# Decay of the third group of chunks loaded and made ahead of the first FFN slot, in a buffer of its own

## The chip, the cores and the metric

The kernel runs on one core of a Trainium2 chip. The metric is the device time of one execution in microseconds (us); less is better. The engines are TensorE (PE in the rows), VectorE (DVE), ScalarE (ACT), GpSimd (POOL) and SyncE (SP), which issues most of the DMAs. Each runs its own row of instructions in order and waits for the others through semaphores.

## What is computed

Three steps follow each other: a gated linear attention, a dense feed-forward network with SiLU, and a second network in which each token goes to the one of eight experts that its gate prefers.

```
def _attn_ref(q, k, v, f_logit):                    # 4 batches, 8 heads, 768 tokens, 48 channels
    f = 1.0 / (1.0 + np.exp(-f_logit))
    for t in range(S):
        state = f[:, :, t, :, None] * state + np.einsum('bhd,bhe->bhde', k[:, :, t], v[:, :, t])
        y[:, :, t] = np.einsum('bhd,bhde->bhe', q[:, :, t], state)
def _moe_ref(x, w_in, w_out):                       # 3072 tokens, 384 channels, 2048 inside
    h = x @ w_in
    g = h * (1.0 / (1.0 + np.exp(-h)))
    return g @ w_out
def _moe2_ref(x, w_gate, w1, w2):                   # top 1 of 8 experts, 1024 inside
    logits = x @ w_gate
    expert_idx = np.argmax(logits, axis=1)
    ...
        out[mask] = gate_w[mask, None] * (np.maximum(xe @ w1[e], 0.0) @ w2[e])
```

The inputs and the result are fp32.

## The kernel before

**Tiling.** The 3072 tokens are 24 chunks of 128; six chunks are one batch. Every large product is made of three TensorE passes over operands that are split into a high and a low part (`_hi`, `_lo`), so each weight and each activation needs a cast on ScalarE (the high part, L226) and a subtraction on VectorE (the low part, L227). The first network's weights also go through a few shifts and masks on VectorE ahead of that (L199, L295 to L303: TENSOR_SCALAR and SCALAR_TENSOR_TENSOR rows on `in_cv`, `out_cv`). The raw weights come by L219, L221 and L222 (`out_raw`, `in_raw`).

**Attention of a chunk** is seven stages, `att0` to `att6`. `att0` makes the decay: a clamp on VectorE (L317), an exponential (L318) and a logarithm (L319) on ScalarE, together a softplus, and then the split `lfh`, `lfl` (L323, L324). `att1` sums it along the chunk by TensorE (`pl`), takes exponentials `ep`, `en` of it (L346 to L348) and makes `qpad`, `kpad` (L349, L350); it also sends the chunk's last row through DRAM (`ends`, L351) to have it as a column (`a_all`, L353). `att2` transposes (`pq`, `pk`, copied as `qt`, `kt`), `att3` makes the scores `sc` and masks them (`am`, L397, two halves of four heads), `att4` the output `py` and the update `pu`, with which VectorE carries the running `state` on (L453, L455), and `att5` transposes the output (`pt`) into `big` or `xt` (L474, L475), the input of the dense network.

**The dense network** works on groups of two or three chunks: the first group is chunks 0 and 1, the second 2 and 3, the third 4, 5 and 6, the fourth 7, 8 and 9. A group takes 16 slots, one for each 128 of the 2048 inner channels. A slot is `ph` (9 matmuls), its Tanh on ScalarE (`se`, L494), `sg` on VectorE (L496), `gh` on ScalarE (L504), `gl` on VectorE (L505), and two slots later `px`. So slots 0 to 15 are the first group's, with attention of later chunks between them. In the rows of the instructions, `se_0_530` is the Tanh of the first half of a slot.

**What sets the order.** A plan `at(slot, fn, ...)` says in which slot a piece is written; pieces before slot 0 have negative numbers. The order on TensorE is then kept as written. On the other engines and SyncE's queue a scheduler puts the instructions in order, by the order in which they are written and by a modelled time at which their inputs and buffers are there: a piece that is ready early by the model can be lifted far ahead of where it was written. The loads of the decay's input of chunks 0 to 3 have places of their own; from the third group on a group's chunks share one tile `in_f` of which there is one buffer: the next group's loads can go out when the last reader of the tile before is done. The Tanh's activation table is not the one that holds exponential and logarithm, so ScalarE loads a table (ACT_TABLE_LOAD) at each change.

`big` is a buffer of 12,288 bytes on each partition. It holds the inputs `xt0` of the first group, a row of zeros `zrow` from which GpSimd and SyncE fill a table in DRAM between slots 22 and 30, and later other tiles: the gate's turned rows `rt`, and an expert's activations `hh_h`.

The functions `load_chunk`, `att0`, `flip_rows` and the plan at the end of the kernel are what the change touches:

## Time and profile before

| | us |
|---|---|
| time, median of 3 runs (lowest, highest) | 857.92 (856.4, 859.5) |
| the profiled execution | 859.19 |
| its span, first to last instruction | 857.5 |
| TensorE busy in the span | 820.6 |
| VectorE, ScalarE, GpSimd busy | 488.1, 384.2, 109.3 |
| mean granted TensorE clock | 0.98 of full |

The profile is of one execution. TensorE's busy time is an upper figure, as its matmuls are pipelined and their ends are modelled. A granted clock of 1.00 is 2.4 GHz, 0.50 is 1.2 GHz. In a timeline a row is the start in us from the span's begin, the duration, the engine and line, the operation, the tiles written and read, and in brackets how long the engine had been idle before it and what ended that. Rows of one engine overlap slightly, so the distance from start to start is what an instruction takes of the engine.

### The profile page before, as it was taken

The numbers are of one execution on the slowest core, as the hardware profiler recorded it, in microseconds if no ns is written. First come the engines' busy times: TensorE is split into PE (matmuls) and PEld (weight loads), VectorE is DVE, ScalarE is ACT, GpSimd is POOL, SyncE is SP. The second block draws the span as 40 slices with busy tenths as digits, with TensorE's granted clock in tenths as the row PEclk, the third lists the DMA queues.
The fourth block names the chain that finished last, engine by engine and source line by source line (L and its number), as shares of the span: only waits on it lengthen the run. The fifth ranks groups of instructions, "written<-read, shape, count | busy, mean of one in ns | idle before, by whom it ended". The sixth has DMA issues, their size and how long they took to land.

```text
span 857.5 us, 15398 instructions
## 1 busy us (share of the span) xinstructions
PE 820.6 (96%) x5684; PEld 782.8 (91%) x5684; DVE 488.1 (57%) x1288; ACT 384.2 (45%) x803; POOL 109.3 (13%) x144
## 2 busy tenths in 40 slices
PE   6899899999999999999999999998999999999994
PEld 3789899989999999999999999998998999999994
DVE  5999875566655556566566556353455336336520
ACT  5665544353353453344445333355264435435520
POOL 2010000002002001001001001066201110110001
PEclk9699899999999999999999999998999999999998
DMA  9856774313244243353344323114182516525400
GB/s 202 172 150 164 188 227 121 65 38 96 71 99 106 59 101 102 75 103 102 74 94 103 74 56 104 44 39 157 48 298 67 172 61 196 170 79 181 162 26 27
DMA packets 166437, 95.94 MB, mean 112 GB/s; under 512 B 115692, under 2 KB 159965, under 8 KB 166352
## 3 DMA queue, kind: packets, MB, share of 16 engines
q1 hardware_dynamic: 162224, 83.80, 37.5%
q0 software_dynamic: 3280, 9.49, 3.0%
q10 hardware_dynamic: 848, 1.57, 0.6%
q8 instruction: 46, 0.75, 0.4%
q14 instruction: 39, 0.32, 0.1%
HBM read 75.61 MB, written 16.33 MB: 107 GB/s over the span
## 4 chain that ended last, share of the span: by engine, by line
PE 70%; DMA 10%; issue 6%; DVE 5%; ACT 5%; SPq 2%; POOL 1%; POOLq 0%; DVEq 0%; ACTq 0%
PE px L330 19%; PE ph L330 19%; PE po L330 8%; PE p L330 7%; PE py L330 5%; DMA out_dram<-o,oi 3%; DMA f<-in_f_logit_dram 2%; PE sc L330 2%; DMA w_raw<-in_moe_w_dram 2%; PE pl L330 1%; PE plt L330 1%; PE p_r L330 1%; PE pq L335 1%; PE po_r L330 1%; PE pk L335 1%
## 5 line engine op out<-in xcount | busy, mean ns | idle before, releaser
L494 ACT ACTIVATE se<-ph 128x384 f32<-128x384 f32 (+1 forms) x144 | 65.5, 455 | 170.2 <-PE ph L330 162.6
L330 PE MATMUL px<-out_lo,gh 128*128 128x384 f32 x384 | 136.7, 356 | 1.6 <-ACT gh L504 1.6
L496 DVE SCALAR_TENSOR_TENSOR sg<-se,ph 128x384 f32<-128x384 f32 (+1 forms) x144 | 72.9, 506 | 108.5 <-ACT se L494 106.0
L330 PE MATMUL px<-out_hi,gl 128*128 128x384 f32 x384 | 130.3, 339 | 1.2 <-DVE gl L505 1.2
L330 PE MATMUL px<-out_hi,gh 128*128 128x384 f32 x384 | 130.0, 338 | 0.0
L330 PE MATMUL ph<-xtl,in_hi 128*128 128x384 f32 (+1 forms) x384 | 125.8, 327 | 0.8 <-DVE xtl L475 0.8
L330 PE MATMUL ph<-xth,in_hi 128*128 128x384 f32 (+1 forms) x384 | 124.1, 323 | 0.0
L330 PE MATMUL ph<-xth,in_lo 128*128 128x384 f32 (+1 forms) x384 | 123.9, 323 | 0.0
L505 DVE TENSOR_TENSOR gl<-sg,gh 128x384 fp32r<-128x384 f32 (+1 forms) x144 | 79.6, 553 | 37.4 <-ACT gh L504 36.5
L504 ACT CAST gh<-sg 128x384 fp32r<-128x384 f32 (+1 forms) x144 | 68.6, 476 | 64.6 <-DVE sg L496 59.2
L330 PEld LDWEIGHTS px<-out_lo,gh 128*128 128x128 f32 x384 | 72.6, 189 | 4.2 <-ACT gh L504 2.3
L330 PEld LDWEIGHTS px<-out_hi,gl 128*128 128x128 f32 x384 | 72.8, 190 | 1.7 <-DVE gl L505 1.7
L330 PEld LDWEIGHTS ph<-xtl,in_hi 128*128 128x128 f32 x384 | 72.6, 189 | 1.1 <-DVE xtl L475 1.1
L330 PEld LDWEIGHTS ph<-xth,in_lo 128*128 128x128 f32 x384 | 72.6, 189 | 0.0
L330 PEld LDWEIGHTS px<-out_hi,gh 128*128 128x128 f32 x384 | 72.6, 189 | 0.0
L330 PEld LDWEIGHTS ph<-xth,in_hi 128*128 128x128 f32 x384 | 72.5, 189 | 0.0
L330 PE MATMUL po<-w_lo,hh 128*128 128x384 f32 (+6 forms) x200 | 67.8, 339 | 0.0
L330 PE MATMUL po<-w_hi,hh 128*128 128x384 f32 (+6 forms) x200 | 67.2, 336 | 0.0
L330 PE MATMUL po<-w_hi,hl 128*128 128x384 f32 (+6 forms) x200 | 67.2, 336 | 0.0
L226 ACT CAST w_hi<-w_raw 128x384 fp32r<-128x384 f32 x124 | 56.9, 513 | 21.6 <-DMA w_raw<-in_moe_w_dram 19.6
L330 PE MATMUL p<-xsl,w_hi 128*128 128x480 f32 (+6 forms) x168 | 58.5, 348 | 0.0
L330 PE MATMUL p<-xsh,w_hi 128*128 128x480 f32 (+6 forms) x168 | 58.4, 347 | 0.0
(240 smaller groups left out, 1528.4 us busy)
## 6 DMA issues: line engine op xcount, KB each, us to landing
w_raw<-in_moe_w_dram SPq DMA_DIRECT2D x64, 384.0 KB
xs<-big SPq DMA_DIRECT2D x8, 776.0 KB
out_again<-in_moe_w_out_dram SPq DMA_DIRECT2D x16, 384.0 KB
xe<-xs SPq DMA_DIRECT2D x7, 776.0 KB
out_raw<-in_moe_w_out_dram SPq DMA_DIRECT2D x13, 384.0 KB
f<-in_f_logit_dram SPq DMA_DIRECT2D x24, 192.0 KB
k<-in_k_dram SPq DMA_DIRECT2D x24, 192.0 KB
q<-in_q_dram SPq DMA_DIRECT2D x24, 192.0 KB
```

Of the source, the lines that this page charges most:

```text
L226: (keep(nc.scalar.copy) if key == ("w1", 1, 1) and RT > 1 else nc.scalar.copy)(hi[:, h], x)
L330: ins = nc.tensor.matmul(*a, **k)
L335: ins = nc.tensor.transpose(*a, **k)
L494: nc.scalar.activation(e, ph[:, :GT], AF.Tanh, scale=0.5)
L496: nc.vector.scalar_tensor_tensor(out=t, in0=e, scalar=1.0, in1=ph[:, :GT], op0=ALU.add, op1=ALU.mult)
L504: (nc.scalar.copy if g < GACT else nc.vector.tensor_copy)(hi, t)
L505: (nc.gpsimd if (g, i) < LOV else nc.vector).tensor_sub(lo, t, hi.bitcast(F32))
```

## The change

The loads of the third group's decay input move from the slot of its first chunk's loads (-3) to `F3 - 2` = -4, and its clamp, exponential and logarithm from `att0` of chunk 4 (slot 0) to `F3` = -2. They need room while `in_f` still holds chunks 0 and 2, 3. So `big` is cut to 4 x 384 words (6,144 bytes), and a new `side` of 388 + 3 x 384 words (6,160 bytes) holds the row of zeros and, behind it, the third group's three chunks. The tiles that took the place of `big` later take `side` (`rt`) or both (`hh_h`).

```diff
 WE = -6
 WS = -1
 PF = 22
+F3 = -2
 PFD = 1
 PW = (0, 0, 1, 1, 2, 2, 3, 3)
 GACT = 9
...
     qpads = [const.tile([P, H, 64], F32, name=f"qpad{i}") for i in range(2)]
     kpads = [const.tile([P, H, 64], F32, name=f"kpad{i}") for i in range(2)]
     wgc = const.tile([P, KC, E], F32, name="wgc")
-    big = late.tile([P, 6 * 512], F32R, tag="big", name="big")
+    big = late.tile([P, 4 * DM], F32R, tag="big", name="big")
+    side = late.tile([P, ROW + CPG * DM], F32, tag="side", name="side")
     xt0 = [big[:, i * 2 * DM : (i + 1) * 2 * DM].rearrange("p (r c t) -> p r c t", r=2, c=KC) for i in range(2)]
-    zrow = big[:, 4 * DM : 4 * DM + ROW].bitcast(F32)
-    spare = big[:, 5 * DM + 2 : 5 * DM + 3]
+    zrow = side[:, :ROW]
+    spare = side[:, DM + 2 : DM + 3]
+    f_third = side[:, ROW:].rearrange("p (r h d) -> p r h d", r=CPG, h=H)
     BANKS = {0: "haahhaaa", 1: "haahhaaa"}
 
     def use(n, i, name):
...
                 tag = {"f": "sg", "q": "gh", "k": "gh", "v": "gl"}[nm]
                 t = att.tile([P, H, D], F32, tag=tag, name=f"{nm}_{n}", bufs=BUFS[tag])
             elif nm == "f":
-                if n == 0 or n == starts[g] and g > 1:
+                if g == 2:
+                    fb[g] = f_third
+                elif n == 0 or n == starts[g] and g > 1:
                     fb[g] = att.tile([P, CPG, H, D], F32, tag="in_f", name=f"f_{n}")
                 t = fb[g][:, r] if g > 1 else fb[0][:, max(n - 1, 0)]
             else:
...
     ysb = {}
     xt = {}
 
+    def softplus(t):
+        nc.vector.tensor_scalar_max(t, t, FMIN)
+        nc.scalar.activation(t, t, AF.Exp, scale=-1.0)
+        nc.scalar.activation(t, t, AF.Ln, bias=1.0)
+
     def att0(n):
         f = loaded.pop(("f", n))
         g, _ = group_of[n]
-        if g < 2 or n == starts[g]:
-            t = f if g < 2 else fb[g][:, : sizes[g]]
-            nc.vector.tensor_scalar_max(t, t, FMIN)
-            nc.scalar.activation(t, t, AF.Exp, scale=-1.0)
-            nc.scalar.activation(t, t, AF.Ln, bias=1.0)
+        if g < 2:
+            softplus(f)
+        elif g > 2 and n == starts[g]:
+            softplus(fb[g][:, : sizes[g]])
         hi = att.tile([P, DM], F32R, name=f"lfh_{n}", **first_use(n, "lfh", "gl"))
         lo = att.tile([P, DM], F32R, name=f"lfl_{n}", **first_use(n, "lfl", "gl"))
         f2 = f.rearrange("p h d -> p (h d)")
...
         for c in range(KC):
             pe.transpose(pt[:, c * P : (c + 1) * P], r[:, c * P : (c + 1) * P], ident)
         if not turned_rows:
-            turned_rows.append(late.tile([P, 4, KC, P], F32, tag="big", name="rt"))
+            turned_rows.append(late.tile([P, 4, KC, P], F32, tag="side", name="rt"))
         rt = turned_rows[0][:, (starts[g] + t) % 4]
         nc.scalar.copy(rt.rearrange("p c t -> p (c t)"), pt[:, :DM])
         flipped[g, t] = pt, rt
...
         w = HEAD * P
         xt_hl = [att.tile([P, CPG, KC, P], F32R, tag=f"xt{x}", name=f"xe{x}_h", bufs=2) for x in "hl"]
         flat = [x.rearrange("p r c t -> p (r c t)") for x in xt_hl]
-        big = late.tile([P, 8 * DM], F32R, tag="big", name="hh_h")
+        bigs = [late.tile([P, 4 * DM], F32R, tag=x, name=f"hh_{x}") for x in ("big", "side")]
         more = [att.tile([P, DM], F32R, tag=x, name=f"{x}_h") for x in ("ep", "en")]
-        slots = [big[:, i * w : (i + 1) * w] for i in range(8 * DM // w)]
+        slots = [x[:, i * w : (i + 1) * w] for x in bigs for i in range(4 * DM // w)]
         slots += [x[:, KC * w : (KC + 1) * w] for x in flat] + [x[:, :w] for x in more]
         items["head"] = dict(
             nm="h", e=0, w=w, rows=items["rows"],
...
         else:
             if r == 0:
                 for m in range(n, n + sizes[g]):
-                    at(s0, load_chunk, m, "f")
+                    at(F3 - 2 if g == 2 else s0, load_chunk, m, "f")
+                if g == 2:
+                    at(F3, lambda: softplus(f_third))
             at(ld, load_chunk, n, "qk")
         at(ld + 1 if g else LV + n, load_chunk, n, "v")
     for u in range(4):
```

How the instructions stand then. Line numbers of the changed kernel are 5 to 11 higher. VectorE in the prologue, where chunk 0's update of `state` (L453, afterwards L462) was and is; `pu_310` and `pu_311` are the same tile. Before:

```order
L199 TENSOR_SCALAR in_cv<-in_raw 128x384
L453 TENSOR_TENSOR state<-pu_310,a_all 48x4x48 x2
L298 SCALAR_TENSOR_TENSOR in_cv<-in_raw,in_cv 128x384
L301 SCALAR_TENSOR_TENSOR in_cv<-in_raw,in_cv 128x384
L397 TENSOR_TENSOR am_0_355<-sc_0_345,trir 128x512
L397 TENSOR_TENSOR am_1_357<-sc_1_346,trir 128x512
L346 TENSOR_SCALAR ep_381<-pl_378 128x384
L227 TENSOR_TENSOR in_lo<-in_cv,in_hi 128x384
L199 TENSOR_SCALAR out_cv<-out_raw 128x384
L475 TENSOR_TENSOR big<-pt_372,big 128x384
L324 TENSOR_TENSOR lfl_395<-f_130,lfh_394 128x384
```

After:

```order
L204 TENSOR_SCALAR in_cv<-in_raw 128x384
L318 TENSOR_SCALAR side<-side 128x1152
L303 SCALAR_TENSOR_TENSOR in_cv<-in_raw,in_cv 128x384
L306 SCALAR_TENSOR_TENSOR in_cv<-in_raw,in_cv 128x384
L406 TENSOR_TENSOR am_0_356<-sc_0_346,trir 128x512
L406 TENSOR_TENSOR am_1_358<-sc_1_347,trir 128x512
L355 TENSOR_SCALAR ep_382<-pl_379 128x384
L232 TENSOR_TENSOR in_lo<-in_cv,in_hi 128x384
L204 TENSOR_SCALAR out_cv<-out_raw 128x384
L484 TENSOR_TENSOR big<-pt_373,big 128x384
L204 TENSOR_SCALAR in_cv<-in_raw 128x384
L462 TENSOR_TENSOR state<-pu_311,a_all 48x4x48 x2
L333 TENSOR_TENSOR lfl_396<-f_131,lfh_395 128x384
```

The update has moved behind the two masks `am`, `ep`, three narrowing rows and `big`, and the clamp of the new tile `side` stands ahead.

VectorE a little later, from chunk 1's update of `state` (L455, afterwards L464) to the low part of `big`, the last that slot 0's first matmul needs. Before:

```order
L455 TENSOR_TENSOR state<-pu_416,state 48x4x48 x2
L301 SCALAR_TENSOR_TENSOR out_cv<-out_raw,out_cv 128x384
L301 SCALAR_TENSOR_TENSOR in_cv<-in_raw,in_cv 128x384
L227 TENSOR_TENSOR out_lo<-out_cv,out_hi 128x384
L346 TENSOR_SCALAR ep_491<-pl_488 128x384
L227 TENSOR_TENSOR in_lo<-in_cv,in_hi 128x384
L199 TENSOR_SCALAR out_cv<-out_raw 128x384
L475 TENSOR_TENSOR big<-pt_482,big 128x384
```

After:

```order
L306 SCALAR_TENSOR_TENSOR in_cv<-in_raw,in_cv 128x384
L464 TENSOR_TENSOR state<-pu_420,state 48x4x48 x2
L232 TENSOR_TENSOR out_lo<-out_cv,out_hi 128x384
L232 TENSOR_TENSOR in_lo<-in_cv,in_hi 128x384
L204 TENSOR_SCALAR in_cv<-in_raw 128x384 x2
L303 SCALAR_TENSOR_TENSOR in_cv<-in_raw,in_cv 128x384 x2
L355 TENSOR_SCALAR ep_494<-pl_491 128x384
L484 TENSOR_TENSOR big<-pt_485,big 128x384
L318 TENSOR_SCALAR f_1662<-f_1662 128x1152
```

Between the row `state<-pu_...` of chunk 0 and this one the changed kernel has 15 rows (before: 14 with both masks, `ep` and `big` among them), of them now 12 narrowing rows; behind it, `ep` now stands behind six narrowing rows where it stood behind three, and behind `big` the clamp of `f_1662`, the fourth group's tile (L311 to L318 before).

ScalarE around the first two Tanh, `se_0` and `se_1`; `f_429` is the third group's tile before, `f_1662` the fourth group's. Before:

```order
L494 ACT_TABLE_LOAD
L494 ACTIVATE se_0_530<-ph_0_520 128x256
L318 ACTIVATE f_429<-f_429 128x1152
L226 CAST out_hi<-out_cv 128x384
L226 CAST in_hi<-in_cv 128x384
L319 ACT_TABLE_LOAD
L319 ACTIVATE f_429<-f_429 128x1152
L504 CAST gh_0_564<-sg_0_532 128x256
L323 CAST lfh_551<-f_429 128x384
L494 ACT_TABLE_LOAD
L494 ACTIVATE se_1_578<-ph_1_568 128x256
```

After:

```order
L319 ACTIVATE f_1662<-f_1662 128x1152
L231 CAST in_hi<-in_cv 128x384
L503 ACT_TABLE_LOAD
L503 ACTIVATE se_0_533<-ph_0_523 128x256
L320 ACT_TABLE_LOAD
L320 ACTIVATE f_1662<-f_1662 128x1152
L231 CAST in_hi<-in_cv 128x384
L513 CAST gh_0_564<-sg_0_535 128x256
L503 ACT_TABLE_LOAD
L503 ACTIVATE se_1_578<-ph_1_568 128x256
L513 CAST gh_1_633<-sg_1_580 128x256
```

The third group's exponential and logarithm have gone from here (to rows ahead of chunk 1's `en`), and the fourth group's stand in their place, with the three table loads; an `in_hi` stands between that logarithm and `gh_0`. Before, the fourth group's stood between `se_7` and `se_8`, with two table loads that are no longer there.

On SyncE's queue the three loads of `side` stand behind the two `v` of chunks 0 and 1, ahead of `ends`, `k` and `q` of the next chunk; the gate weights `wgc` moved behind these; an `out_raw` moved ahead of the four `a_all`; and where the third group's three loads stood are the fourth group's, the last of them behind two more pairs of `in_raw`.

## Rows read from the trace of the kernel before

**Rows 1.** The page's first part: engine, busy us (share of the span), instructions.

```profile
PE 820.6 (96%) x5684; PEld 782.8 (91%) x5684; DVE 488.1 (57%) x1288; ACT 384.2 (45%) x803; POOL 109.3 (13%) x144
```

**Rows 2.** TensorE's waits, 0 to 140 us: who waits for whom, us, times, longest.

```profile
PE py L330 <- DVE am L397: 5.8, 6, 3.0
```

**Rows 3.** Windows: stretch, its us, busy us (count) per engine, granted clock, DMA, GB/s.

```profile
27.83:41.48 13.65, 11.62 (x71) 10.44 (x70) 12.88 (x29) 9.27 (x16) 1.21 (x2) 0.50 0.96 172
41.48:99.51 58.03, 51.35 (x434) 48.56 (x433) 54.25 (x128) 35.49 (x77) 3.96 (x8) 1.00 0.64 162
99.51:106.34 6.83, 6.83 (x31) 6.83 (x31) 5.92 (x15) 1.97 (x5) 0.31 (x1) 0.50 0.75 218
110.00:115.00 5.00, 4.92 (x38) 4.65 (x37) 5.00 (x14) 3.24 (x9) 0.27 (x1) 1.00 0.92 283
```

**Rows 4.** Timeline of TensorE, prologue: start, us, line, operation, tiles, idle before.

```profile
24.05 0.36 PE L330 MATMUL py<-state,qt 112*128 112x96 f32 x2
25.45 0.42 PE L330 MATMUL py<-v,am 128*128 128x48 f32 x2 [1.04 <-DVE am L397]
26.05 0.42 PE L330 MATMUL py<-v,am 128*128 128x48 f32 x2 [0.17 <-DVE am L397]
...
28.89 0.88 PE L330 MATMUL pu<-v,kpad 128*48 128x48 f32 x16
...
31.67 0.85 PE L335 MATMUL pt<-ident,y 128*128 128x128 f32 x3
...
32.63 0.52 PE L330 MATMUL pl<-lfl,trir 128*128 128x384 f32 x1
35.01 0.58 PE L330 MATMUL ph<-big,in_hi 128*128 128x256 f32 x1 [1.85 <-DVE big L475]
...
41.32 0.44 PE L330 MATMUL py<-state,qt 112*128 112x96 f32 x2
```

**Rows 5.** Timeline of VectorE in the same stretch.

```profile
22.75 0.74 DVE L453 TENSOR_TENSOR state<-pu,a_all 48x192 f32<-48x192 f32 x2
23.52 0.56 DVE L298 SCALAR_TENSOR_TENSOR in_cv<-in_raw,in_cv 128x384 uint32<-128x384 uint32 x1
...
28.05 0.35 DVE L199 TENSOR_SCALAR in_cv<-in_raw 128x384 uint32<-128x384 uint32 x1
28.32 0.55 DVE L350 TENSOR_TENSOR kpad<-k,en 128x384 f32<-128x384 f32 x1
...
30.19 0.73 DVE L455 TENSOR_TENSOR state<-pu,state 48x192 f32<-48x192 f32 x2
...
34.40 0.55 DVE L475 TENSOR_TENSOR big<-pt,big 128x384 fp32r<-128x384 f32 x1
...
37.01 0.75 DVE L317 TENSOR_SCALAR f<-f 128x1152 f32<-128x1152 f32 x1
```

**Rows 6.** Timeline of SyncE's queue: start, us until the queue goes on.

```profile
12.81 2.16 SPq L193 DMA_DIRECT2D v<-in_v_dram  x2
...
19.08 2.36 SPq L353 DMA_DIRECT2D a_all<-ends  x4
```

**Rows 7.** Timeline of ScalarE at slot 0.

```profile
37.33 0.38 ACT L494 ACTIVATE se<-ph 128x256 f32<-128x256 f32 x1 [1.17 <-PE ph L330]
```

**Rows 8.** Timelines of TensorE, VectorE, ScalarE (in this order) at slot 8.

```profile
95.32 0.43 PE L330 MATMUL py<-state,qt 112*128 112x96 f32 x2 [0.87 <-DVE am L397]
...
98.93 0.42 PE L330 MATMUL py<-v,am 128*128 128x48 f32 x2 [3.00 <-DVE am L397]
...
97.38 0.42 DVE L496 SCALAR_TENSOR_TENSOR sg<-se,ph 128x256 f32<-128x256 f32 x1 [2.21 <-ACT se L494]
...
93.19 1.28 ACT L319 ACT_TABLE_LOAD   x1
94.49 1.16 ACT L319 ACTIVATE f<-f 128x1152 f32<-128x1152 f32 x1
95.67 1.28 ACT L494 ACT_TABLE_LOAD   x1
```

## The prediction

> **What bounds the kernel now.** The page comes first: TensorE is busy 96% of the span, VectorE 57%, ScalarE 45% [rows 1]. So a change that moves no matmul can only win or lose where TensorE waits, or where its clock is down. The waits of TensorE up to 140 us come next: the largest group is `py`, the chunk's attention output, waiting for `am`, the masked scores that VectorE makes [rows 2]; its longest wait, 3.00 us, is at slot 8 of the second group of the dense FFN. The windows show what surrounds it. From 41.48 to 99.51 us TensorE works 51.35 of 58.03 us, at full clock; the 6.83 us behind that run at granted clock 0.50, the lower of the two levels (1.2 of 2.4 GHz), as do the 13.65 us of the prologue's end [rows 3]. And VectorE is busy 5.00 of 5.00 us at 110 to 115 and 54.25 of 58.03 in the long stretch: in the first 120 us its row of instructions, not its average of 57%, decides when `am`, `state` and the transposed input `big` are there.
>
> The timelines say what happens at the two places that the change touches. In the prologue, chunk 1's `py` starts at 24.05 and then waits 1.04 and 0.17 us for `am`; slot 0's first matmul, `ph`, starts at 35.01 after 1.85 us of waiting for `big` [rows 4]. Around 95 us the fourth group's decay (exponential, table load, logarithm, table load back) holds ScalarE so that the `se` of slot 8 comes late, VectorE idles 2.21 us for it, and `am`, next in VectorE's row, comes late too [rows 8].
>
> **Part 1, the third group's decay ahead of slot 0.** Its three loads now stand on SyncE's queue directly behind chunk 1's `v`. There two loads of that size hold the queue 2.16 us [rows 6], so three hold it 3.24 us, and `ends`, `k`, `q`, `in_raw` and `a_all` behind them go out later; the gate weights' load was moved behind. `a_all`, issued from 19.08 on, had its reader at 22.75 [rows 5, 6]; with the same distance of 3.67 us and an issue at 22.3, it is there at about 26.0. That alone would cost chunk 1's `state` 3.2 us. But the scheduler has also put this `state` further back on VectorE: between it and its old place now stand the clamp `side` (0.75 busy, some 0.7 to the next row) and the row's stretch from 23.52 to 28.32 without `lfl` (4.80 - 0.47 = 4.33). So `state` starts at 22.75 + 0.7 + 4.33 = 27.8, the late `a_all` is hidden by that, and `py` of chunk 1 starts near 28.5 and not at 24.05. Its old waits of 1.21 us for `am` are gone, as `am` now comes first: `pu` starts at 28.5 + (28.89 - 24.05) - 1.21 = 32.1, 3.2 us late, and is done by 33.1.
>
> That is not what decides slot 0, though; VectorE's row is. Four rows of the usual 128x384 kind took 28.32 to 30.19, so 0.47 us each; a TENSOR_SCALAR of 0.35 is followed after 0.27 [rows 5]. Behind `state` (done 28.5) the new row has nine rows of 0.47, two of 0.27 and four of 0.47 until the next `state`: 4.23 + 0.54 + 1.88 = 6.65, so that one starts at 35.15 where it stood at 30.19. `pt` waits for it (35.9, where it was 31.67), and with the 1.48 us from `pt` to the end of `pl` [rows 4] the decay sums stand at 37.4. VectorE by then is still at out_lo, in_lo, two TENSOR_SCALAR and two more shifts (0.94 + 0.54 + 0.94 = 2.42), so that `ep` starts at 38.3, `big` at 38.8, and `ph` of slot 0 at 39.4 and not 35.01: **+4.35 us**. Two of those narrowings read weights whose loads now stand behind three more on the queue; they may wait between nothing and one load's place, 1.08 us. I take the middle. Term 1: **+4.85** (4.35 to 5.45).
>
> **Part 2, what stands at slot 0 now.** The change means to take the exponential, the logarithm and the table switches away from the first Tanh. The order shows that it doesn't: the buffer of the loads comes free once chunk 3 is done with it, and the scheduler lifts the FOURTH group's loads and decay into the place that the third's had. The three table loads around `se_0` and `se_1` stay. What is new is an `in_hi` narrowed on ScalarE behind that logarithm, whose `in_lo` stands on VectorE ahead of chunk 2's first `am`. With X the start of slot 0: clamp X+0.7, exponential to X+1.85 (1.16, as the logarithm's row), `in_hi` to X+2.35, table load to X+3.65, `se_0` to X+4.0, table load to X+5.3, logarithm to X+6.45, `in_hi` to X+6.95, then on VectorE `in_lo` to X+7.45, a TENSOR_SCALAR, `am` to X+8.3, `gl`, a TENSOR_SCALAR, and the second `am` to X+9.6 (durations: [rows 5, 7, 8]). TensorE, by the rows of before, reaches chunk 2's `py` 41.32 - 35.01 = 6.31 after X [rows 4] and needs the first `am` at X+6.6, the second some 0.4 later. It waits 1.7 and then about 0.95. Term 2: **+2.65**; nothing, if ScalarE gets there earlier than this walk, as it did in time before; 4.65, if the clamp waits for its load, the last of which stands behind two more weight loads than the third group's did (up to 2 us, two places). The stage also has lower clock to pay: before, it fell at 27.83, with the first waits, and rose at 41.48 [rows 3]. With waits of 4 us ahead and 2.65 within, it can hardly rise sooner after X than it did (6.5 us); some 6 us of work that ran at full clock may run at half: 0 to 3, I take **+1.5** (term 3).
>
> **Part 3, between slot 1 and slot 15.** From 41.48 to 99.51 TensorE was idle 6.68 us, 3.87 of them at slot 8's `am`, so 2.8 in small waits. The weights are narrowed further ahead now and a later TensorE meets fewer of these: 0 to -2.8. VectorE has hardly any slack to make it up, so I take **-1.0** (term 4).
>
> **Part 4, the stall at 95 us.** The fourth group's decay is gone from there with its two table loads, 1.16 + 1.28 + 1.16 + 1.28 us of ScalarE. The first `am` stood 0.87 late and the second 3.00 [rows 8]. `am` still stands behind `sg` of slot 8, and now behind a TENSOR_SCALAR and a shift too: `se` 0.4, `sg` 0.35, 0.27 and 0.47 while `sc` runs, then twice 0.6, leaves a wait of about 1.2. Term 5: **-2.7** (-3.87 to -1.7). The clock: it fell after these 3.87 us of waiting and cost 6.83 / 2 = 3.4 us [rows 3]. If it no longer falls that comes back, but against a VectorE that is busy 5.00 of 5.00 us at 110 to 115 [rows 3], so between none and all of it is handed back; I put that at 2, a little over half. Term 6: between 0 and -3.4; a fall and no fall being about as likely, I take half of the net 1.4, **-0.7**.
>
> After each load the rows show ScalarE's next ACTIVATE within 0.02 us: 93.19 + 1.28 = 94.47, and 94.49 [rows 8]. The Trainium skill ("ScalarE: Activation LUTs", "What ACT_TABLE_LOAD costs") gives a switch about 2.66 us, the load and a drain, and its section on table sets asks to batch by set, which this change does for one group. By it two switches fewer would be 5.3 us of ScalarE and not 2.56; the trace shows no such drain, and the sum goes by the rows.
>
> **Other edits.** The split of `big` changes names; TensorE's and GpSimd's rows keep their order. The third group's softplus was three instructions and stays three. The turned rows of the gate now use the side buffer, whose last reader before them is the same set of fills: 0.
>
> **The sum.** 4.85 + 2.65 + 1.5 - 1.0 - 2.7 - 0.7 = **+4.6 us** on the profiled execution's 859.19, so 863.8. The three runs have a median of 857.92, 1.27 lower, which gives **862.5**. What a measurement of this kernel can tell from no change is about 0.3%, 2.6 us either way: 855.3 to 860.5. The ends of the terms, each other at its taken value, put the time between 860 and 866.
>
> **Rivals.** *The batch wins.* The two table loads and the stall at slot 8 go as a whole (3.87, and 3.4 of clock, so -7.3), and the prologue costs only what slot 0 loses, 4.35, as ScalarE reaches chunk 2's `in_hi` in time (term 2 and 3 nothing) and term 4 gives its 1.0: 857.92 + 4.35 - 1.0 - 7.3 = 854.0. It decides if `am` of chunk 2 is there within 6.6 us of slot 0's start and the clock does not fall after 99 us. For it: the clock held at full through the small waits of 41 to 99 us. Against it: two table loads and a logarithm ahead of `in_hi`. This is also how the table-set rule of the Trainium skill would have it. Chance 0.13. *The change cancels itself.* It does not do what it says, as the fourth group's decay takes the third's place; what slot 0 loses (4.85, and 1.1 at `am`) is what slot 8 gains (2.7, 3.4 less half of it handed back, and 1.0): about 858.5. Chance 0.19. *Loads late.* VectorE's row waits in front of slot 0 and at the clamp for loads that stand behind the three new ones: 2 us more in term 2, 0.6 in term 1, and the low clock lasts (1.5 more), with no clock gain at slot 8 (0.7): 867.3. Chance 0.13, the upper end of the forecast's side. The forecast itself: 0.55.
>
> **How the numbers follow.** Slower by over 0.3%: 0.55 + 0.13 = 0.68. Within 0.3%: 0.19. Faster: 0.13. The range leaves out the first rival's lower half and the last one's upper part: 856.0 to 867.5; the forecast's own is 860 to 866.
>
> **What would show it.** Step 1: chunk 1's `py` starts near 28.5, waiting for VectorE's `state` and not for `am`; `ph` of slot 0 starts at 39 to 41, waiting for `big`. Step 2: three table loads with a 128x1152 exponential and logarithm stand around the first two `se`, and `py` of chunk 2 waits 1 to 4 us for `am`. Step 3: the low-clock stretch ends behind 46. Step 5: ScalarE has two table loads fewer, and no wait of 3 us at `am` of chunk 5. Wrong would be the sum if slot 0 starts before 38, or if `py` of chunk 2 starts without waiting; or if TensorE, late by 5 us at slot 7, is back in step by slot 12.

## The result, and the profile after

The changed kernel takes **866.73 us** (median of 6 runs, 863.44 to 867.52), the kernel before 857.34 in the runs beside it (6 runs, 856.25 to 859.5). The ratio is 1.0097, with a 95% interval of 1.0081 to 1.0113: slower by about 9 us. That is on the side that was forecast and inside the whole range (856.0 to 867.5), but above the forecast's own (860 to 866) and twice the sum. The profiled execution took 867.52 us.

The page of the changed kernel, first lines: span, then busy us, share and instructions of each engine.

```profile
span 865.8 us, 15398 instructions
...
PE 826.8 (95%) x5684; PEld 790.3 (91%) x5684; DVE 489.1 (56%) x1288; ACT 382.2 (44%) x801; POOL 109.6 (13%) x144
```

Beside [rows 1] this is the most telling line. The number of matmuls is the same, 5684, but TensorE is busy 6.2 us longer; only 2.1 of the span's 8.3 us more are idle time. The same matmuls last longer, so the granted clock is where to look. These are net figures of the whole span: up to chunk 2's `pu` (44.30 us before, 56.15 after) TensorE is idle 8.0 us longer and works 3.9 us longer (34.50 and 38.38), and much of the idle time is given back later. Windows over the low-clock stretches of the first 200 us, and the long one at full clock between them (columns as in [rows 3]):

```profile
27.34:37.58 10.24, 8.68 (x52) 8.45 (x53) 9.89 (x23) 4.37 (x10) 1.21 (x2) 0.50 0.79 177
...
40.99:61.47 20.48, 17.30 (x95) 16.27 (x96) 14.80 (x34) 12.59 (x20) 1.21 (x2) 0.50 0.53 136
61.47:109.26 47.79, 45.28 (x383) 43.99 (x382) 46.77 (x112) 24.66 (x61) 2.79 (x7) 1.00 0.59 162
109.26:116.08 6.82, 6.82 (x28) 6.82 (x28) 5.80 (x15) 2.61 (x8) 0.39 (x1) 0.50 0.81 261
187.76:194.59 6.83, 6.56 (x27) 6.29 (x29) 2.02 (x5) 1.22 (x3) 0.00 (x0) 0.50 0.01 2
```

Before, the prologue's low clock was one stretch of 13.65 us that ended at 41.48 [rows 3]; now there are 30.7 us of it, up to 61.47. The one behind slot 8 is as long as before, and one at 188 us is new. TensorE's waits up to 140 us, who waits for whom, us in total, times, longest:

```profile
PE py L339 <- DVE state L462: 4.5, 1, 4.5
PE py L339 <- DVE am L406: 4.3, 4, 1.6
PE ph L339 <- DVE big L484: 4.2, 1, 4.2
```

The wait of 3.0 us for `am` [rows 2] is gone, as the change wanted; two of over 4 us, for `state` and `big`, have come. The timeline of TensorE has them at chunk 1's `py` and at slot 0's `ph`, to be read against [rows 4]:

```profile
28.90 0.71 PE L339 MATMUL py<-state,qt 112*128 112x96 f32 x2 [4.45 <-DVE state L462]
...
34.15 0.88 PE L339 MATMUL pu<-v,kpad 128*48 128x48 f32 x16
...
42.21 0.58 PE L339 MATMUL ph<-big,in_hi 128*128 128x256 f32 x1 [4.24 <-DVE big L484]
...
48.53 0.57 PE L339 MATMUL py<-state,qt 112*128 112x96 f32 x2
50.52 0.66 PE L339 MATMUL py<-v,am 128*128 128x48 f32 x2 [1.42 <-DVE am L406]
51.72 0.66 PE L339 MATMUL py<-v,am 128*128 128x48 f32 x2 [0.54 <-DVE am L406]
...
56.15 0.88 PE L339 MATMUL pu<-v,kpad 128*48 128x48 f32 x16
```

VectorE's timeline shows what they wait for; compare [rows 5]:

```profile
28.01 0.74 DVE L462 TENSOR_TENSOR state<-pu,a_all 48x192 f32<-48x192 f32 x2
...
35.74 0.74 DVE L464 TENSOR_TENSOR state<-pu,state 48x192 f32<-48x192 f32 x2
...
39.81 0.36 DVE L204 TENSOR_SCALAR in_cv<-in_raw 128x384 uint32<-128x384 uint32 x1 [1.49 <-DMA in_raw<-in_moe_w_in_dram]
...
41.61 0.55 DVE L484 TENSOR_TENSOR big<-pt,big 128x384 fp32r<-128x384 f32 x1
...
49.03 0.56 DVE L232 TENSOR_TENSOR in_lo<-in_cv,in_hi 128x384 fp32r<-128x384 f32 x1 [2.46 <-ACT in_hi L231]
```

And the chain of waits, start and us of two pieces in the prologue, says that both `state` and the narrowing ahead of `big` hang on a transfer:

```profile
23.02 4.96 DMA a_all<-ends
...
35.40 4.29 DMA in_raw<-in_moe_w_in_dram
```

`a_all` went out at 23.02 and was there at 27.98, three hundredths before `state` began; VectorE was done with its row ahead of `state` at 27.93, so the two came almost together. Before, `a_all` went out from 19.08 on, and the one on the chain took 3.00. On ScalarE, around slot 0's Tanh, the fourth group's exponential, the table load, its logarithm and the narrowing behind them:

```profile
42.86 1.17 ACT L319 ACTIVATE f<-f 128x1152 f32<-128x1152 f32 x1
...
46.14 1.28 ACT L320 ACT_TABLE_LOAD   x1
47.44 1.16 ACT L320 ACTIVATE f<-f 128x1152 f32<-128x1152 f32 x1
48.51 0.50 ACT L231 CAST in_hi<-in_cv 128x384 fp32r<-128x384 f32 x1
```

So the change gives the third group's place at slot 0 to the fourth group, as read from the order. How late TensorE runs, at the same instructions of the two timelines:

| instruction on TensorE | before | after | later by |
|---|---|---|---|
| chunk 1's `py` | 24.05 | 28.90 | 4.85 |
| slot 0's `ph` | 35.01 | 42.21 | 7.20 |
| chunk 2's `pu` | 44.30 | 56.15 | 11.85 |
| chunk 5's `sc` (slot 8) | 93.29 | 104.40 | 11.11 |
| chunk 5's `py` | 95.32 | 107.19 | 11.87 |
| first `px` behind it | 102.71 | 110.59 | 7.88 |
| a `ph` behind both low-clock stretches | 119.18 | 127.66 | 8.48 |
| gate's `plt` | 179.03 | 188.03 | 9.00 |
| end of span | 857.5 | 865.8 | 8.3 |

### The profile page after: what moved, and what is told of

Same layout as the page of the kernel before. It is cut to its first block, busy times and chain, and to the rows that moved or that the text cites. A ratio compares the mean times of both kernels' runs of the same rounds, so it can differ in the third digit from the quotient of the medians.

```text
span 865.8 us, 15398 instructions
## 1 busy us (share of the span) xinstructions
PE 826.8 (95%) x5684; PEld 790.3 (91%) x5684; DVE 489.1 (56%) x1288; ACT 382.2 (44%) x801; POOL 109.6 (13%) x144
## 4 chain that ended last, share of the span: by engine, by line
PE 61%; DMA 13%; issue 13%; DVE 8%; ACT 2%; SPq 1%; POOL 1%; POOLq 0%; DVEq 0%; ACTq 0%
PE ph L339 20%; PE px L339 20%; DMA out_dram<-o,oi 8%; PE py L339 5%; PE p L339 2%; PE sc L339 2%; PE po L339 2%; PE plt L339 1%; DMA f<-in_f_logit_dram 1%; PE pl L339 1%; PE p_r L339 1%; PE pq L344 1%; PE po_r L339 1%; PE pk L344 1%; PE plt L344 1%
## 5 line engine op out<-in xcount | busy, mean ns | idle before, releaser
L231 ACT CAST w_hi<-w_raw 128x384 fp32r<-128x384 f32 x124 | 57.2, 514 | 20.5 <-DMA w_raw<-in_moe_w_dram 18.2
```

What stands on the lines that cost most here:

```text
L231: (keep(nc.scalar.copy) if key == ("w1", 1, 1) and RT > 1 else nc.scalar.copy)(hi[:, h], x)
```

## The experiments

Two theories stood against each other. **Loads**: the third group's three loads of 192 KB, ahead of `a_all` and of the weights, make both late, and TensorE's waits and the clock follow. **Decay**: what costs is the work that moved, the clamp and the scheduler's order on VectorE, or the fourth group's decay at slot 0. In the diffs `...` marks what is left out. All ratios are to the kernel before on the same chip, with 95% intervals.

**The split of the buffer alone** (`e5_split_alone`): both groups' loads held where they were, by a small write that depends on the low part of an earlier chunk.

```diff
...
+        if n == starts[2] - 1:
+            nc.gpsimd.tensor_copy(f_third[:, :, 0, 0], lo[:, :CPG].bitcast(F32))
+        if n == starts[3] - 1:
+            fb[3] = att.tile([P, CPG, H, D], F32, tag="in_f", name=f"f_{n + 1}")
+            nc.gpsimd.tensor_copy(fb[3][:, :, 0, 0], lo[:, :CPG].bitcast(F32))
...
-                    at(F3 - 2 if g == 2 else s0, load_chunk, m, "f")
+                    at(s0, load_chunk, m, "f")
...
```

> The buffers of the change and the third group's tile in the side buffer, but its loads are held until chunk 3's split and the fourth group's until chunk 6's split, and the decays are where they were: all that is left of the change is the split of the buffer. Theory: no difference, 855 to 860. Rival (the turned rows of the gate, which now take the side buffer, or the new tiles cost something after 140 us, where four of five changed kernels showed a longer wait for rt and a low clock near 185 us): 860 to 862, with that wait at 2.3 to 2.5 us.

858.25 us (10 runs), ratio 1.0008 (0.999 to 1.0025). Neither the buffers nor the way of holding loads back cost anything that can be measured; the wait for `rt` is 2.1 us here. In its profile chunk 2's `pu` starts at 47.07, 2.8 us later than in that of the kernel before, though the time is the same: a lateness of that size at one place says little of the time.

**The loads alone** (`e3_loads_alone`): the kernel before with the split, the third group in its old tile, and three loads that nobody reads.

```diff
...
+    def extra(m):
+        nc.sync.dma_start(out=f_third[:, m - 4], in_=f_logit[0, :, m * P - 4 * P : m * P - 3 * P, :].rearrange("h p d -> p h d"))
+
+    for m in (4, 5, 6):
+        at(F3 - 2, extra, m)
```

> The kernel before in all but one thing: the side buffer is there and three loads of 192 KB into it go out where the change has them, and nobody reads them; the third group's decay comes through its old tile and old loads. Theory: these loads alone make a_all and the weights late: chunk 1's py near 28.5 to 29, slot 0 at 41 to 42.5, total 862 to 868. Rival (the clamp and the order on VectorE, or ScalarE's early decay, cost it): slot 0 at 35 to 37, total 857 to 860.

864.21 us (4 runs), ratio 1.0097 (1.0062 to 1.0132): as large a loss as the change's, without its early decay. Two rows of VectorE's timeline and two of TensorE's:

```profile
28.41 0.74 DVE L460 TENSOR_TENSOR state<-pu,a_all 48x192 f32<-48x192 f32 x2 [0.33 <-DMA a_all<-ends]
...
33.92 0.76 DVE L316 TENSOR_SCALAR f<-f 128x1152 f32<-128x1152 f32 x1 [0.89 <-DMA f<-in_f_logit_dram]
...
29.30 0.71 PE L337 MATMUL py<-state,qt 112*128 112x96 f32 x2 [5.11 <-DVE state L460]
...
41.12 0.39 PE L337 MATMUL ph<-big,in_hi 128*128 128x256 f32 x1 [1.77 <-DVE big L482]
```

Here VectorE has no early clamp, is done with its row ahead of `state` at 28.08, and stands idle 0.33 us for `a_all`. So early loads are enough for a loss of this size. Two things stay open. In this kernel, too, the scheduler has put `state` behind `am`, and row and transfer end within 0.33 us of each other, so either alone would have kept chunk 1's `py` near 29; no run has the loads early and the old order. And it is not the same loss place by place: the third group's old loads come as well (192 KB, three times), VectorE waited 0.89 us for them at the clamp, chunk 2's `pu` was 5.8 us late where the change's was 11.85, and slot 8 still waits for `am`, 4.3 us at the longest.

**The change without the fourth group's move** (`e1_fourth_held`): only the second of the two holds above.

> The third group's decay is early as in the change, but the fourth group's loads are held until chunk 6's split is made, so its decay goes back to slot 8. Theory (the three loads ahead of a_all and the weights cost the prologue its 7 us): slot 0 still starts near 42, chunk 2's py no longer waits for am, the low clock ends a few us sooner, the stall at slot 8 is back (about 3.9 us and the low clock behind it). Total 863 to 868. Rival (what hurts is the fourth group's decay that has moved to slot 0): 858 to 860, with slot 0 near 36.

864.53 us (4 runs), ratio 1.0091 (1.0062 to 1.0121). Slot 0 starts at 41.67, chunk 2's `py` runs without a wait for `am` to speak of, and slot 8 stalls again, for longer than before:

```profile
105.97 0.71 PE L342 MATMUL py<-state,qt 112*128 112x96 f32 x2 [4.43 <-DVE am L409]
```

Against the change this is no measurable difference: what the fourth group's decay costs at slot 0 it saves at slot 8, within the noise. The low clock ran without a break from 26.71 to 57.44 us here, so it ended 4 us sooner than in the change (61.47).

**Only the fourth group's move** (`e2_third_late`): the first hold alone, the third group's decay in chunk 4's first stage.

> The third group has its own buffer, but its loads are held until chunk 3's split, as in the kernel before, and its decay is in the first stage of chunk 4; only the fourth group's decay is free to move up. Theory: slot 0 starts at 35 to 36 as before; ScalarE makes four table loads around slots 0 to 2, so a wait of 1 to 4 us for am or gh there; the stall at slot 8 is gone (-4 to -7). Total 854 to 858. Rival (the fourth group's place at slot 0 to 2 is the chief cost): 861 or more.

862.11 us (6 runs), ratio 1.0058 (1.0031 to 1.0085): a miss. Slot 0 did start at 36.23 and chunk 5's `py` waited only 1.33 and 0.36 us for `am`. But chunk 2's `pu` came 3.8 us late (slot 0 itself 1.2, two waits for `am` of 1.49 and 0.18 us, and work at half clock), and the clock was low for 23.9 us of the first 54, not 13.65. What slot 8 gave back (2.9 us: chunk 5's `py` 4.4 late, the `px` behind it 1.5) was less than what was lost by then. ScalarE made five table loads from slot 0 to slot 2 (three before), but the last two only at 47.85 and 52.53, about when that `pu` started (48.13) and behind it, so they are not what made it late.

**The loads behind `a_all`** (`e4_after_a_all`): as `e1_fourth_held`, and the loads wait for a write that reads chunk 1's `a_all`.

```diff
+                if g == 2:
+                    at(F3 - 2, lambda: nc.gpsimd.tensor_copy(f_third[:64, :, 0, 0], a_all[:64, 1, :CPG]))
```

> The change, but the third group's loads wait until chunk 1's a_all has landed, and the fourth group is held as in the first run. Theory: a_all and chunk 1's weights are as early as before, so slot 0 at 35 to 37; only one table load stands at slot 0; the stall at slot 8 is as before. Total 855 to 860. Rival (any load of the third group ahead of slot 0 pushes the weights that slot 0 needs): slot 0 at 38 or later, total above 861.

863.89 us (4 runs), ratio 1.0074 (1.0045 to 1.0104). Half a hit: slot 0 starts as before, with one table load at it, and yet chunk 2's `pu` is 3.8 us late, and the time is not measurably better than that of `e1_fourth_held` (1.0091). So giving slot 0 its old start did not by itself bring the total back.

```profile
35.27 0.58 PE L342 MATMUL ph<-big,in_hi 128*128 128x256 f32 x1 [2.00 <-DVE big L487]
...
48.09 0.88 PE L342 MATMUL pu<-v,kpad 128*48 128x48 f32 x16
```

From the windows: the clock is low from 27.33 to 51.23 without a break, TensorE busy 21.07 of these 23.90 us.

```profile
27.33:51.23 23.90, 21.07 (x125) 19.35 (x124) 21.70 (x50) 12.72 (x27) 2.42 (x4) 0.50 0.73 167
```

**The clock kept up** (`e7_change_warm`): the change, with matmuls of a constant into the bank that the waiting instruction is about to overwrite.

```diff
+    def warm(bank, n):
+        for _ in range(n):
+            pe.matmul(bank, ones, ones[:, None, :].to_broadcast([P, 4, P]), start=True, stop=True)
...
+        warm(py, {1: 18, 2: 7, 5: 6}.get(n, 0))
...
+        warm(ph, 18 if (g, i) == (0, 0) else 0)
```

> The change, with TensorE kept busy where it waits: 18 throw-away matmuls of 512 columns into the bank of py ahead of chunk 1's py, 18 into the bank of ph ahead of slot 0, 7 and 6 ahead of py of chunks 2 and 5, each sized to the wait that stands there. The waits stay; only the clock can change. Theory (most of the loss is work at half clock behind the waits: TensorE's busy time rose by 6.2 of the 8.3 us): the low-clock stretches from 27 to 61 us shrink or go, 858 to 862. Rival (the lost time is the waits themselves): 864 to 869.

862.08 us (6 runs), ratio 1.0032 (0.999 to 1.0074), where the change had 1.0097. The waits are still there: slot 0's own matmuls begin at 41.98, where they began at 42.21. But chunk 2's `pu` is at 51.70 and not at 56.15.

```profile
37.26 4.06 PE L339 MATMUL ph<-ones 128*128 128x512 bf16 x18
41.98 0.39 PE L339 MATMUL ph<-big,in_hi 128*128 128x256 f32 x1 [0.66 <-DVE big L489]
...
51.70 0.88 PE L339 MATMUL pu<-v,kpad 128*48 128x48 f32 x16
```

The windows have one low-clock stretch left up to 150 us, from 51.71 to 55.12. Between slot 0 and chunk 2's `pu` lie 9.72 us where the change has 13.94, 4.22 less. Not all of that is the clock, though: with the throw-away matmuls the scheduler changed ScalarE's order, too. Both activations of the fourth group's decay now stand ahead of the first Tanh, with one table load behind them, where the change has three around the first two:

```profile
42.63 1.17 ACT L319 ACTIVATE f<-f 128x1152 f32<-128x1152 f32 x1 [0.52 <-DVE f L318]
...
44.10 1.17 ACT L320 ACTIVATE f<-f 128x1152 f32<-128x1152 f32 x1
...
45.69 1.28 ACT L509 ACT_TABLE_LOAD   x1
46.98 0.38 ACT L509 ACTIVATE se<-ph 128x256 f32<-128x256 f32 x1
```

VectorE's first `am` starts 5.75 us after slot 0 (47.73), 7.57 in the change (49.78), so up to 1.8 of the 4.2 us may come from the order. What is read without it is the work itself: the two `ph` and the `sc` from slot 0 to chunk 2's `py` took 6.32 us in the change (42.21 to 48.53) and take 3.52 here (41.98 to 45.50). In the kernel before they took 6.31 (35.01 to 41.32), so part of what this run gives back is not the change's loss at all. By the medians the run gives back 4.65 of the change's 9.4 us, half of the loss; by the two ratios two thirds (0.65 of 0.97%), and the interval goes from a quarter to the whole. How much of it is the clock is not separated.

**The same for the kernel before** (`e8_before_warm`: 4, 7 and 15 such matmuls ahead of chunk 1's `py`, slot 0 and chunk 5's `py`) **and for the fourth run** (`e12_after_a_all_warm`: 4, 3, 12 ahead of `py` of chunks 1, 2, 5 and 7 ahead of slot 0).

> The kernel before, with 4 such matmuls ahead of chunk 1's py, 7 ahead of slot 0 and 15 ahead of chunk 5's py, each within the wait that stands there. Theory: the low clock of 27.8 to 41.5 and of 99.5 to 106.3 us shrinks or goes; its 18.4 us of work cost up to 9, of which VectorE's row gives back part: 850 to 856. Rival (VectorE sets the time there and the clock costs nothing): 856 to 859.

857.11 us (10 runs), ratio 0.9988 (0.9965 to 1.001): no gain. The stretch behind slot 8 went, but the prologue's low clock only split (28.99 to 35.82, 42.65 to 49.47) and one at 179 us came; up to 200 us the sum of the low-clock time is what it was, 20.5 us. The order on VectorE and ScalarE changed here as well. Whether the kernel before would gain from a full clock stays open.

> The fourth run (third group's loads behind a_all, fourth group's held) with throw-away matmuls in TensorE's waits: 4, 3 and 12 of them ahead of py of chunks 1, 2 and 5, 7 ahead of slot 0. That run started slot 0 at 35.3 as the kernel before and was still 6 us slower, with the low clock up to 51 and from 102 to 113 us. Theory (that excess is the clock): 855 to 859, with less low clock. Rival (it is the order of the work, or the weights behind the loads): 862 to 865 with the clock up.

860.89 us (12 runs), ratio 1.0033 (1.0016 to 1.0051), 3 us below the run without them by the medians, and a good half of that run's excess by the ratios; chunk 2's `pu` is at 42.92, earlier than before. VectorE's and ScalarE's orders differ from that run's as well, so here, too, the clock's part is not separated. Some 0.3% stays, whose place is not known.

**The loads on another engine's queue** (`e6_other_queue` on ScalarE's, as in the diff, `e11_gpsimd_queue` on GpSimd's):

```diff
-            nc.sync.dma_start(out=t, in_=src[b, :, c * P : (c + 1) * P, :].rearrange("h p d -> p h d"))
+            (nc.scalar if nm == "f" and g == 2 else nc.sync).dma_start(out=t, in_=src[b, :, c * P : (c + 1) * P, :].rearrange("h p d -> p h d"))
```

> The change, with the third group's three loads issued by ScalarE and not by SyncE: the same bytes at the same time, but nothing stands behind them on SyncE's queue. Theory (the transfers themselves, which all share the same DMA engines, make a_all and the weights late): little better than the change, chunk 1's py at 27 to 29, slot 0 at 40 to 42, total 862 to 867. Rival (the places on SyncE's queue are what costs): chunk 1's py near 25, slot 0 at 36 to 38, total 857 to 861.

> The change, with the third group's three loads issued by GpSimd, which is idle then: ScalarE is not held by issuing them, and nothing stands behind them on SyncE's queue. VectorE's order stays that of the change, so the time can hardly fall; what is asked is when chunk 1's a_all goes out and lands (19.5 and 22.5 us before, 23.0 and 28.0 with the change). Theory (both: the queue sends it out later, and the transfers that share the DMA engines take longer): out near 20, landed at 24 to 26, total 862 to 867. Rival (the queue alone): landed by 23, in time for the old place on VectorE.

865.93 us (4 runs), 1.0099 (1.0073 to 1.0124), and 867.08 us (4 runs), 1.012 (1.0077 to 1.0163). Neither helps, but neither settles how much is the queue and how much the transfers: on these queues the loads went out sooner still, from 7.4 and 5.1 us on where SyncE had sent them from 14.9 on, beside the first chunks' own inputs, and everything behind ran late: already the first `sc`, at 16.08 before, by 3.3 and 3.9 us. They do show that a queue of its own does not make these loads free: `a_all` went out at 25.06 and 25.89, later still than with the change, and from 5 to 15 us, where the loads now went, the mean busy share of the DMA engines was 1.25 to 1.29 already in the kernel before. What the windows of the first two kernels say of 20 to 25 us, mean busy share of the DMA engines and GB/s at the end, the kernel before and then the changed one:

```profile
20.00:25.00 5.00, 4.38 (x53) 3.98 (x53) 4.22 (x10) 1.41 (x5) 0.00 (x0) 1.00 0.77 126
```

```profile
20.00:25.00 5.00, 4.18 (x51) 3.63 (x51) 4.32 (x10) 2.57 (x6) 0.00 (x0) 1.00 1.20 197
```

Before, the DMA engines were less busy from 20 us on, when `a_all` travelled (0.77); in the changed kernel they are nearly as busy there (1.20) as from 5 to 15.

**A better version?** (`e9_joint`): both decays made together at slot 0, their four activations kept in the order exponential, exponential, logarithm, logarithm; `e10_joint_warm` is the same with 4, 7, 4 and 5 throw-away matmuls.

```diff
...
+        for t in ts:
+            ins = nc.scalar.activation(t, t, AF.Exp, scale=-1.0)
+            if len(ts) > 1:
+                tc.keep_in_program_order(ins)
+        for t in ts:
+            ins = nc.scalar.activation(t, t, AF.Ln, bias=1.0)
+            if len(ts) > 1:
+                tc.keep_in_program_order(ins)
...
-        elif g > 2 and n == starts[g]:
+        elif g == 2 and n == starts[g]:
+            softplus(f_third, fb[3])
+        elif g > 3 and n == starts[g]:
...
```

> The third group's loads held until chunk 3's split, as before, the fourth group's beside them, and both decays made together at slot 0: exponential, exponential, one table load, logarithm, logarithm, one table load back; nothing at slot 8. Theory: slot 0 at 35 to 36; ScalarE is held 7 instead of 5 us between the first two Tanh, so 2 to 4 us are lost there; the stall at slot 8 (3.9 us and the low clock behind it) is gone. Total 853 to 858. Rival (what is lost at slots 0 to 2 is more than slot 8 gives back, as when the decays came one behind the other): 860 to 863.

> The same with throw-away matmuls where TensorE waits: 4 ahead of chunk 1's py, 7 ahead of slot 0, 4 and 5 ahead of py of chunks 2 and 5. Theory: with the clock kept up, 850 to 856, the fastest of all. Rival (VectorE's row sets the time): as without them.

861.13 us (12 runs), 1.0033 (1.0013 to 1.0053), and 864.54 us (7 runs), 1.0084 (1.0054 to 1.0114): misses. The joint decay frees slot 8 (second row) and pays at chunk 2's `py`, behind slot 0 (first row):

```profile
44.11 0.42 PE L350 MATMUL py<-v,am 128*128 128x48 f32 x2 [2.73 <-DVE am L417]
...
99.58 0.43 PE L350 MATMUL py<-state,qt 112*128 112x96 f32 x2 [1.05 <-DVE am L417]
```

With the throw-away matmuls the scheduler changed ScalarE's and VectorE's orders, and behind both decays one `ph` waited 5.7 us for `in_hi`: an edit on TensorE's row that was meant for the clock alone came back as another order elsewhere. No version that was run beats the kernel before.

## Why the prediction was right, and where its sizes were off

The direction, the two places and the mechanism were right; the sum was half of what came. Two thirds of the shortfall are in one term, the first. Terms as the prediction put them, us, against the lateness of TensorE:

| term | forecast | measured | from |
|---|---|---|---|
| 1, start of slot 0 | +4.85 | +7.20 | `ph` 35.01, 42.21 |
| 2 and 3, chunk 2's `am` and the low clock | +4.15 | +4.65 | to `pu`, 11.85 - 7.20 |
| 4, slots 1 to 7 | -1.0 | -0.74 | to slot 8's `sc`, 11.11 |
| 5 and 6, slot 8 and its clock | -3.4 | -2.63 | to the `ph` behind both low-clock stretches, 8.48 |
| behind 119 us | 0 | -0.2 | to the span's end, 8.3 |

**Term 1 is the step that failed.** Its first half stood: `state` at 28.01 (27.8 was forecast), chunk 1's `py` at 28.90 (28.5). Its reason stood less well. The prediction sent `a_all` out at 22.3 and let it take the distance of before, 3.67 us, so that it was "hidden"; it went out at 23.02, took 4.96 and landed at 27.98, as late as VectorE's row, and in `e3_loads_alone` it was the later of the two by 0.33 us. From there the walk down VectorE's row had 35.15 for the next `state` (35.74), and then ep at 38.3, where it was 41.14. Between the two lie a wait of 1.49 us for `in_raw`, which the prediction had bounded at 1.08 and taken at half, and out_lo and in_lo that took 1.45 us (36.51 to 37.96) for the 0.94 of the usual pitch. The bound went by the load's place on the queue, but the load was not what had changed: it went out at 35.40, 0.8 us later than its counterpart before (34.59), and travelled 4.29 us, where one on the chain of the kernel before took 4.05. What had changed is the row that reads it, the fifth of its kind. In the kernel before it stood at 45.56, far behind slot 0's `ph`; now the scheduler has it at 39.81, ahead of `ep` and `big`.

**Terms 2 and 3** came out near their sum by luck, one smaller and one larger than taken. The walk was right: the two `py` that need `am` started 8.31 and 9.51 us after slot 0, where 8.3 and 9.6 had been worked out, behind the very chain that was named (two table loads and a logarithm ahead of `in_hi`, VectorE 2.46 us idle for it). `py` waited only 1.42 and 0.54 us, 1.96 against 2.65, as TensorE came later. The other 2.7 us are half clock: from its first row to `pu`, chunk 2's `py` took 2.98 us before (41.32 to 44.30) and 7.62 now, 5.66 without the waits. 1.5 had been taken. The low clock ended at 61.47, where "behind 46" was forecast, and cost more behind `pu`, as the next term shows.

**Term 4** was about right, and its two parts more so than its sum. From `pu` to slot 8's `sc`, before and after:

```profile
44.30:93.29 48.99, 46.17 (x386) 43.84 (x385) 47.93 (x115) 27.67 (x67) 3.96 (x8) 1.00 0.67 162
```

```profile
56.15:104.40 48.25, 47.37 (x385) 46.17 (x385) 45.03 (x107) 25.66 (x63) 4.00 (x9) 0.94 0.57 157
```

TensorE's small waits fell from 2.82 to 0.88 us, 1.94 less, inside the 0 to 2.8 that the prediction gave; 1.20 us of that went into longer work, at half clock up to 61.47. With it term 3 is 3.9 us and above its range of 0 to 3.

**Term 5** was right to half a us: the stall of 3.87 shrank to one wait of 1.63, -2.24 where -2.7 was taken:

```profile
107.19 0.43 PE L339 MATMUL py<-state,qt 112*128 112x96 f32 x2 [1.63 <-DVE am L406]
```

**Term 6**, the even chance on the clock, fell the dear way: it was low for 6.82 us all the same, though TensorE had waited 1.63 and not 3.87; what is left for this term is -0.4, where -0.7 was taken. So of the 3.7 us by which the profiled executions differ more than the sum said (8.3 and 4.6), 2.35 are term 1, and no other row is off by more than 0.8. By the medians the loss is 9.4 us. The range had a slip of its own: the ends of the terms, each other at its taken value, reach 864.5 (term 2 at 4.65) and not 866.

**What was not forecast** is the stretch at 188 us. It stands behind the gate's first wait for `rt`, before and after:

```profile
179.03 0.83 PE L330 MATMUL plt<-wgc,rt 128*128 128x8 f32 x6 [1.99 <-ACT rt L570]
```

```profile
188.03 1.45 PE L339 MATMUL plt<-wgc,rt 128*128 128x8 f32 x6 [2.52 <-ACT rt L579]
```

TensorE's lateness rose there from 9.0 to 12.0 us. It fell again by 1.7 us up to 590 us, and by 2.4 between 590 and 615, where the clock was low for 3.41 us and in the kernel before for 6.83; at the end of the span it was 8.3. Since `e5_split_alone` has a wait of 2.1 there without a fall of the clock, and is as fast as the kernel before, this is not the new place of `rt`.

**The rivals.** *The batch wins* was out: `py` of chunk 2 waited 1.96 us for `am`, and the clock fell at slot 8. *The change cancels itself* had the fourth group's place right, as the forecast had, but not the balance: 11.85 us were lost by chunk 2's `pu`, and 3.4 had come back behind slot 8's clock. The Trainium skill's rule to batch activations by table set ("ScalarE: Activation LUTs", "Table sets: the hidden batching unit") was carried further in `e9_joint`, in which six chunks share one pair of table loads. That saved the slot 8 stall, but chunk 2's `py` waited 2.73 us for `am`, and the run was slower (1.0033): in this kernel the measurement is against more batching. *Loads late* named loads that stand behind the three new ones, which is near to what came (true of `a_all`, of `in_raw` only in part), at a price of 867.3, against 866.73; that the two agree so closely is luck. It put 5.45 on term 1 (7.20 came) and 4.65 on term 2 (1.96), and the wait at the clamp that it counted on did not come (the clamp of `f` at 42.08 did not wait for its load). It had been given 0.13, no more than the rival on the other side, although the windows of before speak for it: at 15 to 20 us the DMA engines' mean busy share is 1.28 at 183 GB/s, and three more loads of 192 KB are, as an estimate at that rate, 3.2 us that spill into the time in which `a_all` travelled.

## What to carry to other kernels

A load that is moved ahead can be paid by a small transfer that stands behind it, here 0.8 KB (`a_all`, 3.00 us before and 4.96 after): look at the DMA engines' busy share where the new load will travel, and at who waits for the smallest transfer there, before calling it hidden. Moving work out of a place where a list scheduler packs by readiness leaves a hole that something else may take, as the fourth group's decay did here; read the new order, not the diff, and read it again for every experiment, as throw-away matmuls moved it, too. And count a wait of TensorE twice in the sum, once as idle time and once as the work at half clock behind it; up to chunk 2's `pu` the second was half of the first here (3.9 and 8.0 us), and by the end of the span, when most of the idle time had been given back, three times as large (6.2 and 2.1).

## What the runs showed of the hardware

The clock's falls are only loosely tied to the size of the wait ahead of them. At the gate's first wait for `rt` the profiles have waits of 1.7 to 2.9 us; the clock fell there in the kernels with 1.7, 2.1 and 2.3 to 2.9 us (ten), and stayed up in four with 2.0, 2.0, 2.1 and 2.2. So a sum of rows can say what a low stretch costs, but hardly whether it comes, and a fall at that one place made 3 us between the two profiles here (a lateness of 9.0 and then 12.0 us).

In the changed kernel, throw-away matmuls kept the clock up where they filled most of a wait (18 in one of 4.2 us ahead of slot 0), and there they took no time: slot 0 began at 41.98 with them and at 42.21 without. The 18 ahead of chunk 1's `py` did: they began late, at 26.43, after 2.07 us of waiting for `ep`, and that `py` started at 30.31 and not at 28.90, which the wait ahead of slot 0 took up.
